# Transposed softmax weights exchanged through DRAM (one write, four reads) for tiles 6 to 23 of a conformer block, with a rewritten order of all steps

## The chip, the cores and the metric

The kernel runs on one core of one Trainium2 chip. The metric is the device time of one execution in microseconds. Several engines run side by side: PE (TensorE, matrix products), DVE (VectorE), ACT (ScalarE), POOL (GpSimd), and SP (SyncE), which here issues every transfer. PEld is PE's loading of the stationary operand.

## The reference, cut to what matters

Chunked attention with memory keys, then a gated feed-forward block that also mixes along the sequence.

```python
# attention: batch 4, 8 heads, 768 positions, 64 dims; chunks of 32 queries
for c in range(24):
    k_full = concat(mem_k, k[c*32-16 : c*32+40])   # 8 memory keys + up to 56 keys
    a = softmax(q_c @ k_full.T / 8)
    out[:, :, c*32:c*32+32] = a @ v_full
x = out as (4, 768, 512)
# feed-forward
h = gelu_tanh(x @ w_in)                  # 512 -> 1024
u, v = h[..., :512], h[..., 512:]
v_n = layer_norm(v) * g_ln
v_s = einsum('ts,bsd->btd', w_sg, v_n) + b_sg
y = x + (u * v_s) @ w_out
```

All is float32. Each large product is made of three products of high and low parts.

## The kernel before, in words

**Tiles and stages.** Four batches of 768 positions are six tiles of 128 positions each, so there are 24 attention tiles u = 6b + tt. A batch has two halves of three tiles. The work is cut into named steps. A name is a short tag and its tile or block:

- `q8`, `k8`, `v8`: loads for attention tile 8. `S8`: scores, 128 small matmuls into the PSUM tile `s`. `mx8`, `sb8`, `ex8`, `sm8`, `sr8`, `nm8`: row maximum, subtraction (into one of two buffers `e`), exponential (ACT), row sum, reciprocal, and the normalised weights (into the only buffer `n`, on DVE or POOL).
- The weights must be transposed for the next product. Tiles below `PAIRS` do it on PE: `T8` is four 128x128 transposes into a PSUM buffer, and `p8` copies that to `pt` (ACT or DVE). Tiles from `PAIRS` on go another way, two at a time: `yt10`, `yt11` transpose in blocks of 32x32 on DVE into the only buffer `y`, and `Ea5` to `Ed5` (the number is that of the pair) move the blocks from `y` to the right partitions of the only buffer `pt`.
- `A8`: 64 small matmuls of `pt` and `v` into the PSUM tile `av`. `xc8`, `xh8`, `xl8`: copy, high part and low part of the result, the operand of the feed-forward block.
- `V03`: product for the v half, batch 0, tile 3 (12 matmuls of 512 columns), with `v1` to `v9` and `vx`, `vy` behind it: gelu, layer norm, high and low part in `vh`. `U012`: product for the u half, batch 0, half 1, block 2 (12 matmuls of 384 columns), with gelu `u1` to `u4`. `W012`: mixing along the sequence (18 matmuls of 384 columns), which needs all six `vh` of its batch. `w1` to `w4` gate its result. `O012`: output product (12 matmuls), `o1` adds x, `out` stores.
- Weights: `ri12` loads a piece of `w_in` (half 1 serves V, half 0 serves U), and `d1` to `d6` take it apart into high and low parts on ACT, DVE and POOL. `g`, `ga`, `gb` do the same for `w_sg`, and `ro0` to `ro3` with their `d` steps for `w_out`. The pieces of `w_out` land in `y`, since `raw_o` is the same memory.
- `zz10`: ten matmuls without use, which fill PE while it waits at the start.

**Order.** `ORDER` is written out by hand. The program walks it once, and each engine executes its own steps in that order; `InOrder` keeps it so. A star takes the second of the engines that a step allows (for instance POOL in place of DVE for `nm`). Waits between engines come from the data: a step that writes a buffer waits until those that read it are done. So SP, in order too, stops at the first transfer whose data or buffer is not ready, and all transfers behind it stop with it.

**Buffers that link the steps.** `y`, `n`, `pt`, `s` and `av` exist once; `e`, `q`, `k` twice; `v` three times; PSUM has four buffers `mm` for the results of T, V, U, W, O. `yt12` overwrites `y` and thus waits for what reads pair 5 from it; `nm13` overwrites `n` and waits for `yt12`; `sb15` overwrites an `e` and waits for `nm13`; `S16` overwrites `s` and waits for `sb15`. Pair 6's transfers overwrite `pt` and wait for `A11`. One exchange of the kernel before is 16 transfers of 32 partitions by 1 KB from `y` to `pt`, four for each of Ea to Ed.

## Time and profile before

| | |
|---|---|
| median of three runs | 388.61 us (386.21, 388.61, 388.74) |
| the profiled execution | 386.81 us |
| its span, first to last instruction | 385.0 us |
| mean granted TensorE clock in it | 0.989 |
| instructions | 11079 |
| busy: PE, DVE, ACT, POOL | 97%, 65%, 40%, 33% of the span |
| moved by DMA | 47.64 MB, 46.94 MB of it by SP's queue |

Times in the views of the profile are microseconds from the start of the span. All steps are recorded on one line of the program (L105), so they are told apart by the tiles that they write and read, written out<-in, with the letter of the buffer: `mmc<-w_sg_hi,vha` belongs to a W step, `mmb<-paira,w_in_hi` to U, `mmb<-w_in_hi,paira` to V, `mma<-paira,w_out_hi` to O. "[0.92 <-ACT xa]" behind a row says that the engine sat idle for 0.92 us before it, until that instruction was done. In the view of stretches, a column holds the busy time of one engine, then the granted clock of PE, the mean busy share of 16 DMA engines, and the rate in GB/s.

### The profile page before, as it was taken

The page shows a single profiled execution, that of the slowest core. Times are in us where ns is not written, and L with a number is a line of the kernel's source. Part 1 is how long each engine was busy: PE and PEld are TensorE (multiplying, and loading weights), DVE is VectorE, ACT ScalarE, POOL GpSimd, SP SyncE. Part 2 cuts the span into 40 slices and gives each one's busy share as a digit, 9 for nine tenths or more (in the row PEclk, how much of TensorE's full clock was granted, in tenths as well). Part 3 has the DMA queues.
Part 4 walks back from the last instruction along what each step waited for, and adds up shares of the span by engine and source line. Part 5 has one row for each costly group of instructions (what it writes and reads, how often), then busy time and mean ns, then how long its engine had stood idle before and what let it go on. Part 6 is the DMA issues. An engine that isn't in the chain of part 4 may idle for free.

```text
span 385.0 us, 11079 instructions
## 1 busy us (share of the span) xinstructions
PE 372.0 (97%) x4783; PEld 343.6 (89%) x4783; DVE 251.8 (65%) x464; ACT 155.3 (40%) x296; POOL 128.1 (33%) x149
## 2 busy tenths in 40 slices
PE   7979999999999899999999999999999999999996
PEld 5767888999998799899999988899999978999995
DVE  2998989788884669875733485865653357755532
ACT  3867676654323433551221155450420365422110
POOL 3145666631606502241121158530222244600310
PEclk9999999999999789999999999999999999999999
DMA  7999676264348225423003721342101600000015
GB/s 273 344 359 321 232 246 196 113 227 145 136 96 287 84 51 173 155 96 110 3 15 100 215 83 39 98 138 81 31 2 41 196 33 0 3 0 0 2 39 187
DMA packets 24528, 47.64 MB, mean 124 GB/s; under 512 B 4384, under 2 KB 13600, under 8 KB 24480
## 3 DMA queue, kind: packets, MB, share of 16 engines
q1 hardware_dynamic: 24480, 46.94, 37.1%
q8 instruction: 37, 0.61, 0.7%
q14 instruction: 11, 0.09, 0.1%
HBM read 36.96 MB, written 6.29 MB: 112 GB/s over the span
## 4 chain that ended last, share of the span: by engine, by line
PE 82%; DMA 5%; DVE 4%; SPq 4%; issue 2%; ACT 1%; POOL 1%; DVEq 0%; POOLq 0%; ACTq 0%
PE mmd L105 21%; PE mmb L105 19%; PE mma L105 19%; PE mmc L105 14%; PE av L105 6%; SPq L105 4%; PE s L105 4%; DMA rawc<-in_w_in 2%; DMA vb<-in_vs 2%; DMA pt<-y 1%; POOL na L105 1%; DVE rda L105 0%; DVE y L105 0%; DVE eb L105 0%; DVE rdb L105 0%
## 5 line engine op out<-in xcount | busy, mean ns | idle before, releaser
L105 POOL TENSOR_TENSOR paira<-ug,paira 128x384 fp32r<-128x384 f32 x4 | 4.1, 1016 | 39.7 <-ACT paira L105 39.7
L105 DVE STREAM_TRANSPOSE y<-na 128x512 f32<-128x512 f32 x14 | 9.8, 702 | 6.9 <-DMA pt<-y 3.9
L105 PE MATMUL mma<-vhf 128*128 128x512 f32 x36 | 11.5, 479 | 2.4 <-POOL vhf L105 2.4
L105 DVE SCALAR_TENSOR_TENSOR mmd<-mmd,g_half,b_half 128x384 f32<-128x384 f32 x12 | 7.4, 620 | 8.8 <-PE mmd L105 8.8
L105 DVE SCALAR_TENSOR_TENSOR mmb<-mmb,g_half,b_half 128x384 f32<-128x384 f32 x8 | 5.0, 625 | 11.9 <-PE mmb L105 11.9
L105 PEld LDWEIGHTS av<-pt,vb 64*64 64x64 f32 x512 | 8.6, 134 | 4.0 <-issue 1.4
L105 PEld LDWEIGHTS s<-ka,qa 64*32 64x32 f32 x768 | 8.6, 109 | 3.9 <-issue 1.7
L105 PEld LDWEIGHTS mma<-vhf 128*128 128x128 f32 x36 | 8.2, 234 | 4.3 <-POOL vhf L105 2.4
L105 PE MATMUL s<-ka,qa 64*32 64x64 f32 x768 | 10.6, 231 | 1.3 <-DVE eb L105 1.3
L105 PE MATMUL av<-pt,vb 64*64 64x32 f32 x512 | 9.5, 220 | 2.1 <-DMA vb<-in_vs 1.2
L105 PEld LDWEIGHTS s<-kb,qb 64*32 64x32 f32 x768 | 8.5, 105 | 3.2 <-issue 2.7
L105 PEld LDWEIGHTS av<-pt,vc 64*64 64x64 f32 x512 | 9.1, 145 | 2.4 <-issue 2.3
L105 DVE SCALAR_TENSOR_TENSOR gb<-gb,mmb 128x512 f32<-128x512 f32 x10 | 6.8, 677 | 6.7 <-ACT gb L105 6.6
L105 PE MATMUL mmb<-w_in_hi,paira 128*128 128x512 f32 x40 | 11.1, 399 | 0.0
L105 PE MATMUL s<-kb,qb 64*32 64x64 f32 x768 | 10.6, 224 | 0.5 <-issue 0.5
L105 POOL TENSOR_TENSOR na<-eb,rdb 128x512 f32<-128x512 f32 x4 | 4.3, 1074 | 19.0 <-DVE y L105 15.4
L105 DVE SCALAR_TENSOR_TENSOR mma<-mma,g_half,b_half 128x384 f32<-128x384 f32 x8 | 5.0, 623 | 8.5 <-PE mma L105 8.4
L105 PE MATMUL av<-pt,vc 64*64 64x32 f32 x512 | 10.1, 230 | 0.4 <-issue 0.4
L105 PEld LDWEIGHTS av<-pt,va 64*64 64x64 f32 x512 | 8.5, 134 | 2.2 <-issue 1.8
L105 PE MATMUL av<-pt,va 64*64 64x32 f32 x512 | 9.5, 221 | 0.7 <-issue 0.7
L105 ACT ACTIVATE ga<-ga 128x512 f32<-128x512 f32 x12 | 7.6, 633 | 5.2 <-DVE ga L105 5.1
L105 ACT ACTIVATE eb<-eb 128x512 f32<-128x512 f32 x12 | 7.6, 630 | 5.3 <-DVE eb L105 5.3
(518 smaller groups left out, 1246.5 us busy)
## 6 DMA issues: line engine op xcount, KB each, us to landing
ka<-in_ks SPq DMA_DIRECT2D x12, 368.0 KB, 4.4
kb<-in_ks SPq DMA_DIRECT2D x12, 368.0 KB, 4.5
va<-in_vs SPq DMA_DIRECT2D x8, 512.0 KB, 5.5
vb<-in_vs SPq DMA_DIRECT2D x8, 512.0 KB, 5.4
vc<-in_vs SPq DMA_DIRECT2D x8, 512.0 KB, 3.9
pt<-y SPq DMA_DIRECT2D x112, 32.0 KB, 1.9
qa<-in_qs SPq DMA_DIRECT2D x12, 256.0 KB, 4.5
qb<-in_qs SPq DMA_DIRECT2D x12, 256.0 KB, 5.1
```

The source lines that it names most:

```text
L105: return self.tc.keep_in_program_order(getattr(self.engine, name)(*args, **kw))
```

## The change

Three things change. `PAIRS` goes from 10 to 6, so tiles 6 to 9 lose `T` and `p` and get `yt` and an exchange. The exchange of a pair is a write `Ew` of the whole `y` (128 partitions by 4 KB) to one of two DRAM buffers `d`, and then four reads of 128 partitions by 1 KB each, `Ea` to `Ed`, which wait until the write has landed. And `ORDER` is new as a whole.

```diff
-PAIRS = 10
+PAIRS = 6
...
+    dram = ctx.enter_context(tc.tile_pool(name="dram", bufs=1, space=bass.MemoryType.DRAM))
...
+    d_t = buffers(2, [P, 4, 2 * P], F32, "d", dram)
...
-            def exchange(c):
-                def does(eng):
-                    for h in range(2):
-                        for b_ in range(2):
-                            at = 64 * h + 32 * b_
-                            eng.dma_start(
-                                pt_all[at:at + 32, c], y_t[32 * c:32 * c + 32, h, b_]
-                            )
-                return does
+            d = d_t[u // 2 % 2]
+
+            def spread(eng):
+                eng.dma_start(d, y_t.rearrange("p h b j a q -> p (h b) (j a q)"))
+
+            def gather(c):
+                return lambda eng: eng.dma_start(
+                    pt_all[:, c].rearrange("p j a q -> p (j a q)"),
+                    d[CH * c:CH * c + CH].rearrange("p m x -> m p x"),
+                )
 
             step(f"yt{u}", blocks, vector)
             if j:
+                step(f"Ew{u // 2}", spread, sync)
                 for c in range(4):
-                    step(f"E{'abcd'[c]}{u // 2}", exchange(c), sync)
+                    step(f"E{'abcd'[c]}{u // 2}", gather(c), sync)
```

What PE executes in the old and in the new order, from the start through the first batch (`-` old, `+` new), and the new order around the later exchanges:

```diff
-zz4 zz6 zz2 S0 zz13 zz3 zz7 T0 S1 A0 S2 V00 S3 T1 zz3 A1 T2 zz1 T3 A2 V01 S4 A3 V02 S5 V03 S6 U001 T4 U002 S7
-A4 U003 V04 T5 S8 A5 T6 U000 V05 S9 A6 T7 U012 U011 S10 A7 T8 U013 U010 A8 S11 W001 W002 W003 W011 S12 T9 W000
-W012 S13 A9 W010 O000 O002 O001 S14 O003 W013 S15 V12 U101 V11 O011 A10 S16 A11 U102 V10 S17 U103 O010 O013
-O012 A12
+zz1 zz10 S0 zz11 S1 zz9 S2 zz2 zz8 T0 zz7 A0 S3 T1 V00 A1 T2 S4 A2 T3 zz2 V01 A3 V02 S5 T4 V03 S6 U001 A4 S7
+T5 U000 U002 V04 A5 S8 U003 V05 S9 U010 U012 U013 U011 W002 W003 W012 W010 W013 W000 W001 S10 W011 O001 O002
+S11 A6 O000 O013 A7 S12 O003 O010 S13 O012 O011 A8 S14 A9 V10 V11 V13 A10 S15 A11 U101 V12 S16 V14 A12
...
+A17 V23 U200 V21 V24 U202 S23 A18 V25 U212 A19 U211 U213 U210 A20
```

The new order of SP around pair 3, and of all engines behind the last piece of `w_out`:

```diff
+... g30 q11 k11 ro1 ro2 ro3 v6 Ew3 Ec3 Eb3 Ea3 Ed3 k12 q12 v7 q13 Ew4 v9 out001 k13 Ec4 Ed4 Ea4 Eb4 ...
...
+... d2o3* sr8 w1012 w2012 w1010 w2010 d6o2* d1o3 d3o3 yt6 nm7* yt7 w3012 nm8* W013 W000 w1013 u4011 w1000 sb9
+W001 ...
```

## The prediction

> **What bounds the kernel now.** The page first: which engine is full, and where its clock fell.

> ```profile
> PE 372.0 (97%) x4783; PEld 343.6 (89%) x4783; DVE 251.8 (65%) x464; ACT 155.3 (40%) x296; POOL 128.1 (33%) x149
> PEclk9999999999999789999999999999999999999999
> ```

> PE is busy for 97% of the span, so it is the bound, but some of that is filler and some ran at a low clock: two of 40 slices show 7 and 8 tenths. The view of stretches (columns: PE, PEld, DVE, ACT, POOL busy, clock, DMA share, GB/s) says where PE lacks work:

> ```profile
> 18.00:29.00 11.00, 8.93 (x236) 6.92 (x221) 10.38 (x20) 7.72 (x14) 4.49 (x5) 1.00 1.01 351
> 29.00:79.00 50.00, 47.94 (x1072) 41.36 (x1072) 42.92 (x79) 35.98 (x71) 30.85 (x35) 1.00 0.63 213
> 79.00:118.00 39.00, 39.00 (x531) 37.53 (x518) 30.63 (x56) 14.75 (x28) 12.63 (x13) 1.00 0.51 162
> 118.00:137.50 19.50, 18.20 (x253) 16.45 (x254) 12.30 (x24) 6.50 (x12) 9.51 (x11) 0.82 0.50 164
> 318.00:381.20 63.20, 63.20 (x352) 61.11 (x350) 34.24 (x65) 17.34 (x34) 14.39 (x19) 1.00 0.09 32
> ```

> Up to 29 us DVE (10.38 of 11) and DMA (share 1.01) are full and PE waits for them. Behind 79 PE is gapless but for a few places, of which 118 to 137.5 stands out with a clock of 0.82. The timeline of PE names the gaps, a row of the waits says what held ACT, and the chain of waits tells what stands before the second gap and how long PE's steps then took:

> ```profile
> 128.77 1.44 PE L105 MATMUL av<-pt,vb 64*64 64x32 f32 x64 [0.92 <-ACT xa L105]
> 130.59 1.18 PE L105 MATMUL s<-ka,qa 64*32 64x64 f32 x64 [0.38 <-DVE eb L105]
> 310.47 1.21 PE L105 MATMUL av<-pt,vb 64*64 64x32 f32 x64 [0.47 <-DMA vb<-in_vs]
> ACT xa L105 <- DMA out<-xa: 4.3, 1, 4.3
> 121.60 5.40 DMA pt<-y
> 127.38 0.72 DVE y L105
> 128.17 1.05 POOL na L105
> 129.96 0.59 DVE eb L105
> 131.78 1.86 PE av L105 x64
> 133.64 4.01 PE mmd L105 x12
> 237.24 1.06 PE av L105 x64
> 238.31 0.79 PE s L105 x53
> 241.39 2.78 PE mma L105 x12
> 244.16 2.09 PE mmb L105 x12
> 265.02 3.12 PE mmb L105 x18
> ```

> Read it downward. The last transfer out of y lands at 127.0; then yt12 may overwrite y, nm13 (POOL) follows, later sb15, and S16 starts at 130.59. The other gap is A10 behind xc9, which waited 4.3 us for a store of xa that SP had issued among the 16 transfers. After these 1.30 us of gaps PE is slow: two A steps take 1.44 and 1.86 where the row at 237.24 has 1.06, S16 1.18 for 0.79, a U step 4.01 for 2.09. That is 3.5 us more; the rows overlap by about a tenth each, so I take 3.2. The episode cost 4.5, and with 0.47 at 310 **stalls behind 79 cost 5.0 us**. The last five rows price A, S, V, U (and O), and W.

> **Part 1: T6 to T9 and p6 to p9 go.** The price of a T is the time from its start to the next start on PE.

> ```profile
> 92.54 0.66 PE L105 MATMUL mmd<-ident,na 128*128 128x128 f32 x4
> 92.95 0.42 PE L105 MATMUL mma<-w_sg_hi,vha 128*128 128x384 f32 x1
> 103.40 0.70 DVE L105 STREAM_TRANSPOSE y<-na 128x512 f32<-128x512 f32 x1
> 132.83 10.73 SPq L105 DMA_DIRECT2D pt<-y  x16
> pt<-y SPq DMA_DIRECT2D x112, 32.0 KB, 1.9
> out<-xa SPq DMA_DIRECT2D x12, 192.0 KB, 2.2
> vc<-in_vs SPq DMA_DIRECT2D x8, 512.0 KB, 3.9
> ```

> 4 x 0.41 = **-1.6 us**, all of it on PE where PE is gapless. The four yt add 4 x 0.70 = 2.8 us to DVE, at W and O steps (30.63 busy of 39 there): hidden, and worth at most its own length if that cover were gone.

> **Part 2: the exchange.** Before, SP issues 16 transfers in 10.73 us and the last lands 1.9 later: 12.6 us, and y is held that long. Now Ew lands, then four gathers are issued 0.67 apart (10.73/16). The trace has no write of 512 KB; the nearest rows are 2.2 (192 KB stored) and 3.9 (512 KB loaded), and I take 3.0. A gather of 128 KB lies between 1.9 (32 KB) and 2.2 (192 KB); I take 2.2, nearest in size. So the exchange takes 0.4 + 3.0 + 3 x 0.67 + 2.2 = 7.6 us, and y is free after 3.4. SP spends 5 x 0.67 = 3.4 us on issues and about 3.0 standing before the first gather, 6.4 for 10.7. Behind that new wait stand k12, q12 (S12), then v7, q13, Ew4; S12 is reached 8 us of PE work behind A6, so nothing on PE feels it. The chain that ended in S16 shortens by 9 us and the store of xa leaves earlier: I count the stall of **5.0 us as gone** (least 0, if the new order opens an equal one).

> The gathers overwrite pt and wait for the A before. What the new order puts on PE between: A9 to A10 V10 V11 V13 (8.3 us), A11 to A12 U101 V12 S16 V14 (8.4), A19 to A20 U211 U213 U210 (6.2); the other pairs have 12 us and more. Needed: 0.4 + 2.0 + 2.2 = 4.6. Covered, unless a gather is slow, which these rows bound:

> ```profile
> DMA packets 24528, 47.64 MB, mean 124 GB/s; under 512 B 4384, under 2 KB 13600, under 8 KB 24480
> 141.00:143.00 2.00, 2.00 (x36) 1.91 (x19) 1.73 (x3) 1.76 (x4) 0.00 (x0) 1.00 0.22 54
> 5.00:10.00 5.00, 5.00 (x77) 3.59 (x76) 2.56 (x5) 1.77 (x4) 1.27 (x1) 1.00 0.99 371
> ```

> One engine moves 54/(0.22 x 16) = 15.3 GB/s in packets of 1 KB (second row, pt<-y alone) and 23.4 in full loads (third). The source of a gather is four blocks of 32 rows. If it were split along these four, each engine would move 32 KB, 2.1 to 1.4 us a gather, and the four gathers on the same engines 8.4 to 5.6. With 1.5 for issue and landing beyond the transfer, the last comes 9.9 to 7.1 behind the A. A takes its last quarter 0.8 after its start, so the waits are 0.8 + 0.7 + 2.9 = 4.4, or 0.1. I take **+1.0**.

> [...]

> **Part 3: the order at the start.** Both orders have the same steps on PE before V05 but for T6. DVE sets the pace: xl5, which V05 needs, is DVE's 91st step in the new order and the 84th in the old. At 42.92/79 = 0.54 us a step that is 3.8 later than 59.8, if none of DVE's idle time (7.1 of 50) is won back, and PE's own work allows 60.6. I take V05 at 62.0 (was 61.0).

> ```profile
> 61.00 1.20 PE L105 MATMUL mmb<-w_in_hi,pairb 128*128 128x512 f32 x4
> 59.15 0.69 DVE L105 TENSOR_TENSOR pairb<-av,pairb 128x512 fp32r<-128x512 f32 x1 [0.89 <-ACT pairb L105]
> 79.07 0.45 PE L105 MATMUL mmc<-w_sg_hi,vha 128*128 128x384 f32 x1
> 76.67 1.28 POOL L105 TENSOR_TENSOR vhf<-gb,vhf 128x512 fp32r<-128x512 f32 x1 [1.32 <-ACT vhf L105]
> 78.71 0.33 SPq L105 DMA_DIRECT2D y<-in_w_out  x1
> 86.23 8.56 SPq L105 DMA_DIRECT2D y<-in_w_out  x2
> ```

> Then V05, S9 and four U end at 62.0 + 2.8 + 0.8 + 8.4 = 74.0. The old kernel reached W001 at 79.07 with S10, S11, A6 to A8, T6 to T8 (1.6 + 3.2 + 1.2 = 6.0) done besides: 73.1 alike. **+0.9** (from -0.7 to +2.5). W002 needs v9 of tile 5: before, vhf ended 77.95, 14.1 behind V05's end; now PE comes 9.2 behind it and needs that part 0.9 later. The old time was not pressed, since PE had other work until 79.07; by count it is 23 DVE steps, 12.4 us behind xl5, so 74.4 against 74.9. The wait lies between 0 and 4.0; I take **+0.7**. Fillers (50 for 39) fall into PE's waits. Ahead of S4's q and k SP has seven pieces of w_in, five pairs of q and k and three v, where it had four v: the loads are no later.

> **Sum** on the profiled execution's 386.81 (span 385.0): -1.6 - 5.0 + 1.0 + 0.9 + 0.7 = -4.0, so **382.8**. The median of the runs shown is 388.61, 1.8 above that execution, so I say 383.0. A change under 1% (3.9 us) can't be told from none here.

> **The rivals.**

> *Slow gathers.* If they run on few engines at the low rate, A10, A12 and A20 wait 4.4 in place of 1.0, and a gap of 2.9 is longer than the 1.30 that cost 3.2 of slow clock: 382.8 + 3.4 + 3.2 = 389.4 at worst, 387 in the middle. For it speaks the four-block source; against it that 23.4 GB/s leaves 0.1. Chance 0.25.

> *The chain through y at pair 3 (slower).* y is also where w_out lands. Before, ro1 left at 78.71 and the first yt ran at 103.40: 24.7 us. The new order asks yt6 behind the same four pieces, and only then come yt7, Ew3, the gathers and A6. ro1 waits for d1o0, which stands on ACT behind V05 and U010, so about 70; yt6 is then at 94.7, and 0.7 + 1.05 + 0.7 + 7.6 later, at 104.8, pt is there. PE reaches A6 at 74.7 + 3.1 + 27.6 = 105.4. Only 0.6 us lie between. Behind that each us is lost, with 3.2 for the clock once the gap passes that of before. If ro1 leaves at 78.7 as it did, yt6 is at 103.4, A6 waits 8.1, and the time is 394.1; slower by over 1% from yt6 at about 100. Against it: V05, S9 and U010 are over by 68. Chance 0.15.

> *The start.* V05 at 63.6 and a vhf as late as before (14.1) give +1.6 + 3.3: 387.7. Chance 0.10.

> **How the numbers follow.** Forecast 0.50 (own range 380 to 386), slow gathers 0.25, y 0.15, start 0.10. Faster by over 1% means below 384.7: 0.39 + 0.07 + 0.01 + 0.03 = 0.50. Slower (over 392.5): 0.03 + 0.10 + 0.02 = 0.15. The rest, 0.35, is within 1%. The range goes down to 378.5 (no gather wait, start at -0.7, no wait for vhf: 379.5, less 1 for execution spread) and up to 391, which leaves out the worse part of the y rival.

> **What would show it.** T6 to T9 gone: 16 fewer transposes on PE. Exchange: from Ew to the last gather 7.6 us, y free after 3.4; the clock row 9 at slices 13 and 14, and no gap before S16. Engines of a gather: 3312 packets under 512 B if all transfers are 16-way, 2880 if the 36 gathers are 4-way. Start: V05 at 62, W002 at 74, yt6 before 95. Wrong if PE waits before A6 or A20 by over 2 us, or if the new order opens a gap that none of these steps names.

## The result, and the profile after

The changed kernel takes **390.96 us** (median of 11 runs, 389.29 to 395.26) against 386.55 for the kernel before on the same chip (11 runs, 384.56 to 389.45): ratio **1.0116**, 95% interval 1.0072 to 1.016. It is slower by about 4.5 us where 4.0 less was forecast. The profiled execution took 390.65 us, its span is 388.9, its mean granted clock 0.986. Ratios here and below are formed from fast executions alone, so they can differ a little from the quotient of the medians; one execution of an experiment (by block) took 1414.72 us with PE slow throughout (busy for 1406.9 us), and a second profile of that kernel is read in its place.

The page of the kernel after: busy time, the granted clock in 40 slices, and the packets.

```profile
PE 374.1 (96%) x4778; PEld 344.5 (89%) x4778; DVE 255.9 (66%) x475; ACT 153.0 (39%) x289; POOL 122.3 (31%) x145
PEclk9899999999999969999999999999999999999999
DMA packets 25199, 53.39 MB, mean 137 GB/s; under 512 B 2880, under 2 KB 13120, under 8 KB 25152
```

PE was busy 2.1 us longer, though four T's are gone; there are 11 more fillers, and the clock row has an 8 in slice 1 (counted from 0) that the kernel before did not have. Slice 14 shows 6 tenths, where the kernel before had 7 and 8 in slices 13 and 14. The 2880 packets are the number named ahead for gathers on four engines. The count can be made from the traces: the kernel before has 242 transfers, and 16 small packets for each and the 512 single elements of g_half are its 4384 packets under 512 B; the 175 transfers here would make 3312 in the same way, and 36 gathers with 12 fewer each make 2880.

The timeline of PE of the kernel after: the first matmuls of V05, W002 and A6, which the prediction timed, and then the rows behind 125 us with an idle time of 0.4 us or more in front ("<-issue" means that the profile shows nothing that PE waited for).

```profile
61.96 1.08 PE L106 MATMUL mmd<-w_in_hi,pairb 128*128 128x512 f32 x4
...
74.07 0.33 PE L106 MATMUL mma<-w_sg_hi,vha 128*128 128x384 f32 x1
...
105.06 1.14 PE L106 MATMUL av<-pt,va 64*64 64x32 f32 x64
...
134.90 0.43 PE L106 MATMUL av<-pt,vb 64*64 64x32 f32 x16 [1.07 <-DMA pt<-db]
136.34 0.67 PE L106 MATMUL av<-pt,vb 64*64 64x32 f32 x32 [1.00 <-DMA pt<-db]
137.76 0.43 PE L106 MATMUL av<-pt,vb 64*64 64x32 f32 x16 [0.76 <-DMA pt<-db]
...
152.74 0.90 PE L106 MATMUL av<-pt,va 64*64 64x32 f32 x48 [0.44 <-DMA pt<-da]
...
248.04 1.14 PE L106 MATMUL av<-pt,va 64*64 64x32 f32 x64 [0.42 <-issue]
...
263.28 0.43 PE L106 MATMUL av<-pt,vc 64*64 64x32 f32 x16 [0.67 <-DMA pt<-da]
```

The start came as forecast, and A6 ran without a wait. A10 (pair 5) stopped three times for a gather, 2.83 us in all; A12 and A20 stopped 0.44 and 0.67. The 0.42 before A18 has no releaser in the row, but it is a gather too: the last of pair 9 marks its landing at 247.75 to 247.95, and the first matmul of A18 starts at 248.04. Together that is 4.36 us. The view of stretches shows what followed (columns as before: the last three are granted clock, DMA share, GB/s):

```profile
134.00:138.00 4.00, 1.34 (x64) 1.12 (x64) 1.86 (x4) 0.00 (x0) 1.61 (x1) 1.00 0.40 146
138.00:140.00 2.00, 2.00 (x119) 1.83 (x116) 0.91 (x2) 1.62 (x3) 0.56 (x1) 0.70 0.44 122
140.00:142.00 2.00, 2.00 (x40) 1.94 (x33) 1.44 (x3) 1.11 (x2) 1.46 (x3) 0.50 1.18 375
142.00:144.00 2.00, 2.00 (x8) 2.00 (x7) 2.00 (x4) 1.19 (x2) 0.00 (x0) 0.50 0.82 215
144.00:146.00 2.00, 2.00 (x8) 1.77 (x7) 1.90 (x4) 0.06 (x1) 1.28 (x1) 0.59 0.69 224
```

Behind A10 PE is full and slow: 2 x (0.30 + 0.50 + 0.50 + 0.41) = 3.4 us of clock lost. Waits and clock make **7.8 us**, and the span without them would be 388.9 - 7.8 = 381.1.

The chain of waits of the kernel after, only its transfers around pairs 5, 6 and 10, and SP's timeline at pairs 5 and 10:

```profile
121.29 5.25 DMA db<-y
128.90 8.81 DMA pt<-db
143.17 9.53 DMA pt<-da
256.49 6.74 DMA pt<-da
```

```profile
126.61 0.53 SPq L106 DMA_DIRECT2D pt<-db  x1
127.20 0.46 SPq L106 DMA_DIRECT2D vc<-in_vs  x1
127.71 1.72 SPq L106 DMA_DIRECT2D pt<-db  x3
...
254.69 2.31 SPq L106 DMA_DIRECT2D pt<-da  x4
```

The write of pair 5 lands 5.25 us after it was taken up, and the last gather 8.81 after its own issue, at 137.71. For pair 10, with nothing but the load of v21 behind it, the set runs from 254.69 to 263.23: 8.5 us. PE has 8.3 to 8.4 us of work between the A steps of pairs 5 and 6 and 6.2 at pair 10, so none of the three was covered. Pair 9 had 13.5 us and came late all the same: its gathers stand in SP's order behind Ew10 and v19, the last also behind v20 and a store, and they were issued from 236.33 to 239.21, while A17 was over at 234.1.

The trace also shows on how many engines a gather runs. The landing of a load has 16 marks. A gather here has one mark about 1 us after its issue and four at its end, and those of pair 10 end one after the other, at 258.4, 259.9, 261.8 and 263.2. Of the 16 marks of v21's load, twelve stand between 261.35 and 262.06 and four between 264.06 and 264.39, behind the last gather: a quarter of its engines had the gathers to do first.

### The profile page after: what moved, and what is told of

It is laid out like the page before. It is cut to its first block, busy times and chain, and to the rows that moved or that the text cites. A ratio compares the mean times of both kernels' runs of the same rounds, so it can differ in the third digit from the quotient of the medians.

```text
span 388.9 us, 10956 instructions
## 1 busy us (share of the span) xinstructions
PE 374.1 (96%) x4778; PEld 344.5 (89%) x4778; DVE 255.9 (66%) x475; ACT 153.0 (39%) x289; POOL 122.3 (31%) x145
## 2 busy tenths in 40 slices
DMA packets 25199, 53.39 MB, mean 137 GB/s; under 512 B 2880, under 2 KB 13120, under 8 KB 25152
## 4 chain that ended last, share of the span: by engine, by line
PE 78%; DMA 11%; DVE 5%; SPq 2%; issue 2%; POOL 1%; ACT 1%; POOLq 0%; ACTq 0%
PE mma L106 22%; PE mmc L106 18%; PE mmb L106 15%; PE mmd L106 14%; PE av L106 5%; DMA pt<-da 4%; PE s L106 4%; DMA pt<-db 2%; SPq L106 2%; DMA out<-xb 2%; DMA db<-y 1%; DMA uc<-in_w_sgT 1%; DVE w_in_lo L106 0%; DVE gb L106 0%; POOL w_sg_lo L106 0%
## 5 line engine op out<-in xcount | busy, mean ns | idle before, releaser
L106 PE MATMUL mma<-vhf 128*128 128x512 f32 x41 | 13.4, 487 | 2.4 <-POOL vhf L106 2.4
L106 DVE SCALAR_TENSOR_TENSOR mmc<-mmc,g_half,b_half 128x384 f32<-128x384 f32 x9 | 5.6, 624 | 13.7 <-PE mmc L106 13.7
L106 DVE STREAM_TRANSPOSE y<-na 128x512 f32<-128x512 f32 x18 | 12.7, 703 | 3.0 <-POOL na L106 2.4
L106 DVE SCALAR_TENSOR_TENSOR mma<-mma,g_half,b_half 128x384 f32<-128x384 f32 x12 | 7.4, 621 | 9.3 <-PE mma L106 9.2
L106 ACT ACTIVATE ea<-ea 128x512 f32<-128x512 f32 x12 | 7.6, 629 | 12.4 <-DVE ea L106 12.4
L106 DVE SCALAR_TENSOR_TENSOR gb<-gb,mma 128x512 f32<-128x512 f32 x10 | 6.8, 677 | 6.7 <-ACT gb L106 6.7
L106 POOL TENSOR_SCALAR rsa<-mva 128x1 f32<-128x1 f32 x8 | 2.6, 330 | 26.4 <-DVE mva L106 26.4
L106 DVE TENSOR_REDUCE mxa<-s 128x8 f32<-128x512 f32 x8 | 5.4, 681 | 6.6 <-PE s L106 6.6
L106 DVE SCALAR_TENSOR_TENSOR gb<-gb,mmc 128x512 f32<-128x512 f32 x8 | 5.5, 683 | 6.6 <-ACT gb L106 6.6
L106 DVE TENSOR_REDUCE mxc<-s 128x8 f32<-128x512 f32 x8 | 5.5, 683 | 6.1 <-PE s L106 6.1
## 6 DMA issues: line engine op xcount, KB each, us to landing
va<-in_vs SPq DMA_DIRECT2D x8, 512.0 KB
vb<-in_vs SPq DMA_DIRECT2D x8, 512.0 KB
vc<-in_vs SPq DMA_DIRECT2D x8, 512.0 KB
db<-y SPq DMA_DIRECT2D x5, 512.0 KB
```

What stands on the lines that cost most here:

```text
L106: return self.tc.keep_in_program_order(getattr(self.engine, name)(*args, **kw))
```

## The experiments

Theory: **four engines**. The source of a gather has four blocks as its slowest dimension, and its landing has four marks at the end where that of a load has 16: its packets run on four of 16 DMA engines, all four gathers on the same ones, and they come too late where the new order leaves only 6 to 8 us. Rivals: the way over DRAM itself (the write, and the wait for its landing), loads that lie on the same engines, and the new order as such. Ratios are to the kernel before on the same chip.

### The new order with the old exchange

```diff
-                step(f"Ew{u // 2}", spread, sync)
...
+                                pt_all[at:at + 32, c], y_t[32 * c:32 * c + 32, h, b_]
```

PAIRS is 6 and the order is the new one without the Ew. As the new order runs the next yt ahead of some of the old exchange, part of the weights that reach pt are another tile's; the amount of work is the same.

> The new order with the old exchange (16 transfers inside the chip, no Ew). Theory 'four engines': the loss comes from gathers that run on 4 of 16 engines, so the new order alone is not at fault; but this order leaves only 8.3, 8.4 and 6.2 us between the A steps, and the old exchange takes 12.6, so A10, A12 and A20 should wait about 4, 4 and 6 us, with 3.2 us of slow clock behind each: 400 us or more, ratio to before 1.03 or over. Rival 'way over DRAM' (any exchange with two landings is worse than one inside the chip): faster than the changed kernel, ratio below 1.01. Rival 'order' (the new order loses whatever the exchange): about 1.01 as the changed kernel.

Measured: 438.36 us, ratio 1.1306 (1.1262 to 1.135), as expected over 1.03. Two of its 16 waits of PE for pt, from the timeline of PE:

```profile
128.94 0.27 PE L106 MATMUL av<-pt,vc 64*64 64x32 f32 x2 [4.10 <-DMA pt<-y]
...
285.60 2.24 PE L106 MATMUL av<-pt,va 64*64 64x32 f32 x64 [6.80 <-DMA pt<-y]
```

The new order can't do without the new exchange: what follows A asks for y and pt sooner than 16 transfers of one issue each allow. The order alone can't be judged from this kernel.

### The old order with the new exchange

```diff
-... q15 k14 q14 Ed5 k15 ...
+... q15 k14 q14 Ew5 Ed5 k15 ...
```

The diff is against the kernel before. `PAIRS` stays 10, the exchange is that of the changed kernel, one Ew stands in front of the first gather of each pair, and all else is the order before.

> The old order and the old PAIRS = 10 with the new exchange, Ew placed right ahead of each pair's first gather. Theory 'four engines': a gather set needs about 10 us, the old order leaves 14 us or more between the A steps, so PE does not wait for pt; y comes free earlier, so the 4.5 us of gaps and slow clock at 128 us go: ratio 0.988 to 0.998. Rival 'way over DRAM': the standing of SP delays loads, ratio 1.005 or more. Rival 'order': about 1.00.

Measured: 382.55 us, **0.9863** (0.983 to 0.9897), a little better than the expected 0.988 to 0.998. The stretch in which the kernel before stood still and slow (118 to 137.5, there 18.20 busy at a clock of 0.82), in the view of stretches of this kernel:

```profile
118.00:137.50 19.50, 19.50 (x389) 16.91 (x390) 13.45 (x26) 7.20 (x14) 10.75 (x12) 1.00 0.53 183
```

PE is full at full clock, and no wait stands behind 60 us. So the stall that the prediction counted at 5.0 is ended by the exchange alone: 1.37% of 387.89 is 5.3 us. The four-block source is in this kernel too, and PE waits for none of its gathers, since other work covers them.

### All exchanges on 16 engines, in the new order

Ew is cut into four writes, so that the DRAM buffer holds the rows in the order in which a gather wants them, and each gather reads 128 rows in one block.

```diff
-            d = d_t[u // 2 % 2]
+            d = d_t[u // 2 % 2].rearrange("p m x -> (p m) x")
...
-                eng.dma_start(d, y_t.rearrange("p h b j a q -> p (h b) (j a q)"))
+                for c in range(4):
+                    eng.dma_start(
+                        d[P * c:P * c + P].rearrange("(m p) x -> p m x", p=CH),
+                        y_t[CH * c:CH * c + CH].rearrange("p h b j a q -> p (h b) (j a q)"),
+                    )
...
-                    pt_all[:, c].rearrange("p j a q -> p (j a q)"),
-                    d[CH * c:CH * c + CH].rearrange("p m x -> m p x"),
+                    pt_all[:, c].rearrange("p j a q -> p (j a q)"), d[P * c:P * c + P]
```

> The changed kernel with another layout in DRAM: four writes of 32 partitions put each quarter where its gather reads 128 rows in one run, so that every transfer has an outer dimension of 32 or 128. Theory 'four engines': packets under 512 B are all 16-way (3744 in place of 2880), the gaps before A10, A12, A20 go with the slow clock (2.8 + 0.4 + 0.7 + 3.2 = 7.1 us), less a little for three more issues a pair: ratio 0.993 to 0.998. Rival 'way over DRAM': gaps stay, ratio about 1.01. Rival 'order': gaps before other steps, ratio 1.005 or more.

Measured: 383.81 us, **0.991** (0.9876 to 0.9945). Its page has the packets, its timeline of PE the gaps behind 60 us, both of them:

```profile
DMA packets 29519, 53.39 MB, mean 140 GB/s; under 512 B 3744, under 2 KB 18592, under 8 KB 29472
```

```profile
134.24 1.25 PE L106 MATMUL av<-pt,vb 64*64 64x32 f32 x64 [0.45 <-DMA pt<-db]
...
138.41 1.01 PE L106 MATMUL av<-pt,vc 64*64 64x32 f32 x54 [1.80 <-issue]
```

With all 16 engines A10 waits 0.45 in place of 2.83, A12, A18 and A20 not at all, and the clock stays full. From 1.0116 to 0.991 is 2.1%, about 8 us, as much as the 7.8 of waits and clock, and better than the expected 0.993 to 0.998. The way over DRAM is still there, so it isn't what cost the time. A new gap of 1.80 at A11 has no releaser in the profile.

### The same in the old order

> The old order and PAIRS = 10 with the four writes and the 16-way gathers of the run before. Theory 'four engines': as the old order with the new exchange or a little faster, 0.988 to 0.998, since the old order covers the slow gathers too. Rival 'way over DRAM': 1.005 or more. Rival 'order': the same as the old order with the four-way gathers, about 1.00.

Measured: 383.88 us, 0.9879 (0.9838 to 0.9921; 0.988 to 0.998 was expected), not to be told apart from the old order with four engines (0.9863). Where the exchange is covered, the number of engines of a gather makes no difference that these runs show.

### Pair 5 alone on 16 engines

```diff
+            wide = u // 2 == 5
...
+                    rows[P * c:P * c + P] if wide
+                    else d[CH * c:CH * c + CH].rearrange("p m x -> m p x"),
```

> The changed kernel, with pair 5 alone written as four blocks so that each of its gathers reads 128 contiguous rows; the other eight pairs keep the source of four blocks. Theory 'four engines': A10's waits of 2.83 us shrink to about 0.45 (as in the kernel where all pairs are so) and with them the slow clock behind A10 (3.2 us); A12, A14 and A20 keep their 0.44, 0.42 and 0.67. So 5.6 us less: about 385.4 on the scale of 390.96, a ratio to the kernel before near 0.997. Packets under 512 B: 2880 + 4 x 12 + 3 x 16 = 2976. Rival 'the way over DRAM itself' (write under load, waiting for its landing): pair 5 still has it, so A10 still waits over 2 us and the ratio stays at 1.01. Rival 'the new order loses elsewhere': the same, over 1.005.

Measured: 389.1 us, 1.0053 (1.0015 to 1.0091), a gain of 0.6% where 1.4% was expected. From its timeline of PE:

```profile
135.41 1.48 PE L106 MATMUL av<-pt,vb 64*64 64x32 f32 x64 [1.09 <-DMA pt<-db]
...
139.19 1.01 PE L106 MATMUL av<-pt,vc 64*64 64x32 f32 x54 [1.17 <-issue]
...
150.84 0.90 PE L106 MATMUL av<-pt,va 64*64 64x32 f32 x48 [1.43 <-DMA pt<-da]
...
248.35 1.14 PE L106 MATMUL av<-pt,va 64*64 64x32 f32 x64 [1.12 <-DMA pt<-db]
```

The theory was right on the place and wrong on the sum. A10 waits 1.09, not 0.45, and as PE comes to A12 earlier, pair 6, still on four engines, stops it for 1.43 in place of 0.44, with 1.7 us of clock lost behind A12. A18 (called A14 in the expectation) waits 1.12 in place of 0.42, and here the row names the gather of pair 9. A part of the loss moved on to later pairs.

### Loads behind the gathers, and the write one step earlier

Two kernels with the four-block source kept. The first moves the gathers of pair 5 ahead of v11 and k16; the second moves Ew5 ahead of out002 too.

```diff
-... q15 out013 out002 Ew5 v10 ... Ec5 v11 Ea5 Eb5 Ed5 k16 ...
+... q15 out013 out002 Ew5 v10 ... Ea5 Eb5 Ec5 Ed5 v11 k16 ...
+... q15 out013 Ew5 out002 v10 ... Ea5 Eb5 Ec5 Ed5 v11 k16 ...
```

> The changed kernel with one line of the order changed: pair 5's four gathers stand in the order a, b, c, d ahead of the loads v11 and k16 (v11 stood between the first and the second). All exchanges keep their source of four blocks. Theory 'four engines, and loads in front on the same engines': v11's 512 KB no longer lie ahead of three of the gathers, so from the first issue at 126.6 the last lands after about 9.5 in place of 11.1 us, near 136, and A10 waits 1.0 to 1.8 us in place of 2.83; the slow clock behind it gets shorter or goes (0 to 3). Ratio 0.997 to 1.008. Rival 'four engines alone': four gathers on four engines take as long as before, A10 waits 2.5 to 3 and the ratio stays at 1.01. Rival 'contention alone': A10 waits under 0.3 and the clock stays full, ratio near 0.996.

> The changed kernel, source of four blocks kept everywhere; at pair 5 the gathers a, b, c, d stand ahead of v11 and k16, and Ew5 stands one step earlier, ahead of the store out002. Theory 'four engines': a set of four takes 8.5 us from the first issue with nothing beside it (as pair 10's did). The write is issued at 118.4 in place of 121.3 and has landed when A9 ends at 125.2, so the gathers start there and end at 133.7 to 134.7; PE comes to A10 at 133.8 and reads its last quarter 0.8 later. A10 waits 0 to 0.6 us, the clock stays full: 5 to 6 us less than the changed kernel, ratio 0.995 to 0.998. Rival 'the four-block source is slower still when other transfers run': A10 waits over 1.5 us, ratio over 1.005.

Measured: 389.74 us, 1.0093 (1.0054 to 1.0132), and 389.69 us, 1.0084 (1.0044 to 1.0124). The timelines of PE, the first kernel and then the second; then for the second SP's timeline at the gathers, and SP's waits from 118 to 132 us (total, times, longest):

```profile
135.12 0.43 PE L106 MATMUL av<-pt,vb 64*64 64x32 f32 x16 [1.19 <-DMA pt<-db]
136.35 0.43 PE L106 MATMUL av<-pt,vb 64*64 64x32 f32 x16 [0.80 <-DMA pt<-db]
```

```profile
136.79 0.43 PE L106 MATMUL av<-pt,vb 64*64 64x32 f32 x16 [1.35 <-DMA pt<-db]
138.07 0.65 PE L106 MATMUL av<-pt,vb 64*64 64x32 f32 x16 [0.85 <-DMA pt<-db]
```

```profile
127.09 2.33 SPq L106 DMA_DIRECT2D pt<-db  x4
```

```profile
SPq L106 <- DMA db<-y: 1.3, 1, 1.3
```

A10 still waits 1.99 and 2.20, and the slow clock follows. The first kernel misses its expectation by a little (a wait of 1.0 to 1.8, 0.997 to 1.008), the second by much (a wait of 0 to 0.6, 0.995 to 0.998). The write was taken up at 120.61 (118.4 was expected) and landed no sooner than 127.05, 6.4 us later, so its head start was eaten up on the way. And from 127.09 the gathers took until 138.03: 10.9 us, where the expectation had 8.5, though v11 stood behind them. Room in SP's queue saves next to nothing; with loads and stores still under way ahead of it, a set on four engines is slower still.

### The cut of the gather alone

The sharpest test: order, write, bytes, packets of 1 KB, queue and number of transfers are those of the changed kernel, and only the cut of a gather is turned. It takes one block column into 32 partitions in place of four blocks into 128.

```diff
-            def gather(c):
+            def gather(m):
...
-                    pt_all[:, c].rearrange("p j a q -> p (j a q)"),
-                    d[CH * c:CH * c + CH].rearrange("p m x -> m p x"),
+                    pt_all[CH * m:CH * m + CH].rearrange("p c j a q -> p c (j a q)"),
+                    d[:, m].rearrange("(c p) x -> p c x", p=CH),
```

> The changed kernel with its order and its single write, and nothing else changed but the cut of the four gathers: each reads one block column of d, that is 32 rows of 4 x 1 KB into 32 partitions, in place of four blocks of 32 rows into 128 partitions. As many transfers, bytes and packets of 1 KB, on the same queue; the slowest dimension of each side is 32 in place of 4 and 128. Theory 'four engines': all transfers run on 16 engines, so 3312 packets under 512 B, no wait for pt over 0.6 us at A12 and A20 and under 1 at A10, the slow clock behind A10 gone: about 383 to 385, ratio 0.990 to 0.996. Rival 'the write': the earlier 16-way kernel also cut the write into four; if that was the cause, this kernel stays at 1.008 to 1.012 with waits for pt of over 2 us at A10.

> One profile of the kernel with gathers by block column in the order of the changed kernel (its 11 timed executions lie near 385.7, 0.9989 of the kernel before; the profiled one was not usable). Theory 'four engines': 3312 packets under 512 B; no wait for pt at A12, A14 and A20; a last gather that lands under 6 us behind its issue in pair 10 (6.74 with four engines). What keeps it 0.8% above the other 16-way kernel of this order is then to be found at A10 and A11: a wait for pt there, with v11 in front of the gathers, or idle time of PE without a releaser, and a clock under 1 behind it. Rival 'the cut of the gather matters by its place on the partitions': each of 32 partitions by 4 KB is slower than 128 by 1 KB, and waits for pt of over 0.5 us stand at A12 and A20 too.

Measured: 385.85 us, **0.9989** (0.9954 to 1.0025); the second profile took 385.58. Its page, its timeline of PE behind 60 us (all gaps), and its stretches behind A11:

```profile
DMA packets 25631, 53.39 MB, mean 139 GB/s; under 512 B 3312, under 2 KB 13552, under 8 KB 25584
```

```profile
133.95 0.27 PE L106 MATMUL av<-pt,vb 64*64 64x32 f32 x2 [1.19 <-DMA pt<-db]
134.44 1.13 PE L106 MATMUL av<-pt,vb 64*64 64x32 f32 x62 [0.22 <-DMA pt<-db]
...
138.04 1.28 PE L106 MATMUL av<-pt,vc 64*64 64x32 f32 x56 [1.43 <-issue]
```

```profile
138.00:140.00 2.00, 1.96 (x58) 1.90 (x58) 1.44 (x3) 1.25 (x3) 0.82 (x3) 0.65 0.82 293
140.00:142.00 2.00, 2.00 (x8) 2.00 (x8) 1.97 (x5) 0.97 (x2) 0.52 (x1) 0.50 1.01 303
```

The 3312 packets are the number named for 16-way transfers, 12 more for each of the 36 gathers. From 1.0116 to 0.9989 is 1.3%, **4.9 us**, and only the cut of the gather, and with it the number of engines, differs. In the trace each gather now has 16 landing marks at its end. The write is whole here, so the rival of the write falls; and as the other cut to 16 engines, with its 128 partitions, gains too, it is the engines and not the place on the partitions. It is a step less than expected (0.990 to 0.996): A10 still waits 1.41 (under 1 was expected), A11 stops 1.43 without a releaser, and the clock behind loses 1.7; A12, A18 and A20 wait for nothing, as expected. The same set of four at pair 10 in the view of stretches, first the changed kernel from 256, then this one from 253:

```profile
256.00:258.00 2.00, 2.00 (x14) 2.00 (x13) 1.91 (x4) 0.72 (x2) 1.22 (x2) 1.00 0.23 75
258.00:261.00 3.00, 3.00 (x19) 3.00 (x18) 2.33 (x6) 2.24 (x6) 0.57 (x1) 1.00 0.74 208
261.00:263.00 2.00, 1.61 (x53) 1.25 (x51) 1.55 (x3) 0.45 (x1) 0.00 (x0) 1.00 0.38 111
```

```profile
253.00:255.00 2.00, 2.00 (x14) 2.00 (x13) 1.84 (x5) 0.85 (x2) 1.17 (x3) 1.00 0.97 234
255.00:257.00 2.00, 2.00 (x13) 2.00 (x13) 1.41 (x4) 1.39 (x4) 0.12 (x1) 1.00 0.86 248
```

Alone, the gathers fill 0.23 of the DMA, about four engines of 16 (the 0.74 in the middle has the load of v21 beside them). With the other cut the share is 0.97 and 0.86: the first gather is issued at 251.88, the last has landed at 256.40, 4.5 us later (8.5 on four engines), and the load at 258.21.

### Versions that could win

The new order on 16 engines with the two edits of pair 5, once with the write in four and once by block, and the old order by block:

> The kernel with all exchanges on 16 engines in the new order (0.991 of the kernel before, with 0.45 us of wait for pt at A10 and 1.8 behind it), with two more edits of the order at pair 5: gathers a, b, c, d ahead of v11 and k16, and Ew5 one step earlier, ahead of the store out002, which it waited behind. Theory 'four engines': with 16 engines, no load in front and the write landed before A9 ends at 125.2, nothing waits at A10; about 1 to 2 us less than without these edits, ratio 0.987 to 0.990. Rival 'issue of PE' (the gap of 1.8 has nothing to do with the exchange): ratio stays at 0.991. If it falls under 0.986 the new order is better than the old one with the new exchange.

> The new order with gathers by block column, and the two edits at pair 5: gathers ahead of v11 and k16, Ew5 ahead of out002. Theory 'four engines': no wait for pt left, ratio 0.987 to 0.991. If the new order has any gain of its own over the old one (four T's of 0.41 us each are gone), this is where it shows: under 0.986. If it stays at 0.989 the new order is worth nothing more than the old one with the same exchange.

> The old order with tiles 6 to 9 on T as before, the exchange by one write and four gathers cut by block column (32 partitions by 4 x 1 KB). The old order leaves 14 us or more between the A steps of two pairs, so the cut should matter little here: 0.984 to 0.989 of the kernel before, like the two other kernels of the old order with the new exchange (0.9863 and 0.9879). Theory 'four engines' says no more than 0.3% better than these, since there PE waited for no gather.

Measured: 382.89 us, 0.9892 (0.9844 to 0.994); 384.34 us, 0.9944 (0.9908 to 0.998); and 382.01 us, 0.9906 (0.9869 to 0.9942). Neither kernel of the new order has a wait for pt left behind 60 us, only a stop at A11 without a releaser (0.47 and 1.49). The second missed its expectation of 0.987 to 0.991 and the third that of 0.984 to 0.989. The three kernels of the old order with the new exchange have 0.9863, 0.9879 and 0.9906, the three of the new order on 16 engines with the split write or the edits of pair 5 have 0.991, 0.9892 and 0.9944. The intervals overlap; all six beat both the kernel before and the changed one, and nothing shows that the new order is worth anything of its own.

## Why the prediction was wrong, point by point

**The step that failed: "I take +1.0" for the waits of the gathers.** What it stands for measured 7.8 us, 4.36 of waits and 3.4 of clock. It went wrong in the choice between the ends: 0.1 and 4.4 were both worked out for gathers on four engines, and 1.0 was picked near the lower one without a row for it. The sum that called the gathers covered (4.6 us needed) took their landing as 2.2 us, that of a store of 192 KB. A gather is a load from DRAM, and loads near it in size took longer in the kernel before: 2.4 to 5.4 us for pieces of `w_sg` with 192 KB, and 4.5 to 5.1 for q with 256 KB. Two rows of its list of transfers (the last column is the median from issue to landing):

```profile
uc<-in_w_sgT SPq DMA_DIRECT2D x3, 192.0 KB, 3.8
qa<-in_qs SPq DMA_DIRECT2D x12, 256.0 KB, 4.5
```

On four engines the last gather lands 6.74 us after its issue with little beside it and 8.81 and 9.53 among loads. On 16 engines it is still twice the 2.2, in the list of transfers of the kernel with the split write:

```profile
pt<-db SPq DMA_DIRECT2D x20, 128.0 KB, 4.2
pt<-da SPq DMA_DIRECT2D x16, 128.0 KB, 4.4
```

But that was nearly covered: A10 waited 0.45 in this kernel and 1.41 in the one by block, which is about the +1.0. For 16 engines the term would have come out right, by luck, since a landing is about twice the 2.2 there too. With the split write the kernel comes to 0.991, where the forecast's 382.8 on 386.81 is 0.9896; by block, with the stop at A11 and 1.7 us of clock, it comes to 0.9989.

**The rival "slow gathers"** named what came. No transfer of the kernel before showed on how many engines a source of four blocks runs, so its chance of 0.25 was the author's estimate. The pages of the new order agree with the rival, with 2880 packets for the four-block source and 3312 with 32 rows as the slowest dimension. Its price was 389.4 at worst, for 390.65 measured in the profile, and its waits 4.4 for 4.36 measured. That the sums agree is luck, for the waits lay elsewhere: 0.8, 0.7 and 2.9 were expected at A10, A12 and A20, and 2.83, 0.44 and 0.67 came, with 0.42 at A18, which was held to be covered by 12 us and more. At A20 the set was over 7.9 us behind A19, within the 7.1 to 9.9 of the bounds; at A10 it was 12.5 behind A9. Both bounds took engines that have nothing else to do; the 1.5 us for issue and landing in them was the author's estimate. At A10 there were loads and stores to finish first (the DMA share was 0.97 from 122 to 126 us, before the first gather), and v11 stood between the gathers.

**The write** was taken at 3.0. At pair 5 it was 5.25, among v10 and three stores; this delayed the first gather from 125.2 to 126.6. So y was free after 5.25 and not 3.4 us, and from Ew5 to the last gather it took 16.4 and not 7.6, with the wait for A9 in it. The write adds to the wait at A10, but with the same write the kernel by block wins 4.9 us.

**The stall at 127 to 137 us gone, -5.0:** held, and shown alone by the old order with the new exchange (5.3). In the changed kernel the clock row has 9 in slice 13 as named and 6 in slice 14: S16 starts at 148.09 without a gap, so the stall itself is gone, and the gap at A10 cost as much clock as the old one had, 3.4 us. In the kernel before, the clock was halved from 130.53 to 137.36 us; so its A step at 128.77, which the prediction counts as slow, still ran at full clock, but the 3.2 taken in all was near.

**The start, +0.9 and +0.7:** V05 at 61.96 for 62.0, W002 at 74.07, between 74.0 and 74.7. The rival of the start did not come.

**The chain through y at pair 3:** A6 ran at 105.06 without a wait (105.4 forecast). The yt6 that was reckoned at 94.7 at the latest and asked to be before 95 ran at 89.31, so there was more room than 0.6 us.

**T6 to T9, -1.6:** not measured by itself. The six kernels of the two orders with the new exchange don't show that it is left at the end.

**What remains:** without waits for pt and slow clock the span is 381.1, and by the prediction's other terms it is 385.0 - 4.0 - 1.0 = 380.0. Of these 1.1 us, 0.6 are the gaps of 0.31 (S13, for its q) and 0.28 (at 316 us, for a step of DVE); the other 0.5 is not accounted for.

## What to carry to other kernels

In these runs the bytes of a transfer alone did not set its cost: four gathers of 128 KB took 8.5 us with four blocks as the slowest dimension of their source and 4.5 with 32 rows. So before a rearrangement is put on the DMA, try more than one cut of it, and count the small packets of the page (2880 and 3312 here) to see on how many engines it runs. A pipeline that is tightened to the length of its exchange has to be sized by an exchange measured among the other transfers of that moment, since an order with 14 us between two uses hid a difference that cost 1.3% in an order with 8. And when rates from two rows give waits of 4.4 and 0.1 us, ask whether any row excludes one of the ends before taking a value near the other; here none did, and neither row had the traffic of the moment in it.
